# Divisions, readings and stores as operations of their own, and a new order for all operations, in an attention-and-FFN kernel

## The chip, the cores and the metric

The kernel runs on one core of a Trainium2 chip. The metric is the device time of one execution in microseconds (us), lower is better; of several runs the median is given. One core has a matrix engine (TensorE, PE in the profile, with its weight loads shown apart as PEld), three engines that work element by element (VectorE = DVE, ScalarE = ACT, GpSimd = POOL), and a sync engine (SP) that here only issues DMA transfers. Each engine executes its own instructions in program order. An instruction that needs a result of another engine waits on a semaphore, and everything behind it on its engine waits with it.

## The reference, cut to what matters

```python
# q, k, v: (8 batches, 8 heads, 576 positions, 64)
def phi(x, c, s):                          # c, s = cos, sin of pi/2 * position / 576
    r = np.maximum(x, 0.0)
    return np.concatenate([r * c, r * s], axis=-1)
q_p = phi(q, cos_w, sin_w)                 # 128 features
k_p = phi(k, cos_w, sin_w)
kv = np.einsum('bhsf,bhsd->bhfd', k_p, v)
z = np.sum(k_p, axis=2)
num = np.einsum('bhsf,bhfd->bhsd', q_p, kv)
den = np.einsum('bhsf,bhf->bhs', q_p, z)[..., None] + 1e-06
x = (num / den).transpose(0, 2, 1, 3).reshape(4608, 512)
h = x @ w_in                               # 512 -> 2048
out = np.maximum(0.01 * h, h) @ w_out      # 2048 -> 512
```

It is a linear attention (cosFormer), whose output is divided by a row sum, followed by a two-layer network with a leaky ReLU.

## The kernel before, in words

The 4608 tokens are worked in nine groups of 512: group g = 0 to 7 is the first 512 positions of batch g, group 8 gathers the 64 tail positions of all eight batches. A group goes through the same stages.

- *Attention.* q and k go through phi on DVE, ACT or POOL (`q_prep`, `k_cos`, `k_sin`; `q`, `k` in the first two groups). PE sums k_pᵀ[v|1] over positions (`kv_sum`; `kv` in the first groups). q_p is transposed, by PE or by a DMA (`q_transpose_dma`), and PE multiplies it with kv (`num(g,j)`, four blocks j of 128 tokens; `nh(b,jp,hg)` in the first two groups, half-blocks over token pair jp and head half hg). The product holds the numerator and, in one column per head, the denominator.
- *Division* (lines 571 to 576). Three DVE instructions: denominator plus 1e-6 (`den`), its reciprocal (`rden`), and numerator times reciprocal into the tile `xs`. They follow one another in one function `divide`, which `num` calls itself and `dh` calls for the half-blocks.
- *Transpose of x.* `xs` becomes `xT`, through PE in the first three groups (`xh`, `x_transpose`), through a DMA on SP's queue from group 3 on (`x_transpose_dma`, line 524).
- *FFN1.* Plain matmuls for groups 0 to 2 (`h`, `M`; line 634). From group 3 on a scheme with seven products in place of eight: `P(g,u,n)` is product n of column part u (line 787), `e(g,u,x)` are the steps that read the products and apply the leaky ReLU, `x_sum(g,i)` the sums of quarters of x that it needs (tiles X1, X2, X4, X1b).
- *FFN2.* Plain for group 0 (`f2(tt,lo,hi)`, line 661: token block tt, rows lo to hi of the 16 parts of the hidden width). From group 1 on seven products again: `F(g,i)` is half i of the seven products' halves, four matmuls of 128x256 each (line 904). `g_sum` are the sums of quarters of the hidden layer. When a product's last half is done, the same call reads it (lines 687, 923, 932: into t1, t2, t3 inside `ext`, or into the output tile `osb`) and issues the store of the finished quarter (`store_quarter`, line 963 and 968; for group 8's last quarters `store_tail`, line 954). Quarters have the product numbers 2, 4, 3 and 5.

PSUM (the matmul accumulators) is given out from four small pools; `osb` has four buffers. Loads are issued on SP's queue, as are the DMA transposes and the stores; half of group 8's stores go through ACT's queue.

What sets the order is one long text, `PROGRAM`: a list of some thousand operations with the engine letter of each (D, A, P). The kernel is built by calling the operations in that order, so each engine's instructions stand in the order of the text, and a semaphore joins what depends on one another across engines. `idle(n)` puts in n matmuls on a blank tile. w_in and w_out are loaded in parts and cast to 16 bits by `w1(i,c,n,engine)` and `w2(i,engine)`; `w2` part i covers hidden parts 4i to 4i+3. `load(...)` in the text is a transfer on SP's queue.

Of the kernel before, what the change touches and what calls it, by code (L numbers as in the profile page):

```python
# [9 lines left out]
dt = mybir.dt  # L10
# [3 lines left out]
P = 128  # L14
J = 4
# [10 lines left out]
q(0,0,0,4,D) q(0,1,0,4,D) q(0,2,0,4,D) q(0,3,0,4,A) q(0,0,4,8,D) q(0,1,4,8,D) q(0,2,4,8,P) q(0,3,4,8,A)  # L26
k(0,0,1,c,D) k(0,0,1,s,D) k(0,1,2,c,D) k(0,1,2,s,D) qT(0,0,A,h) idle(1,o) qT(0,1,A,h) idle(1,o) v(0,0,1,A)
v(0,1,2,A) qT(0,2,A,n) idle(1,o) qT(0,3,D,h) idle(6,o) kvps(0,h) kv(0,0,2) kvo(0,0,2,A) k(0,2,4,c,P,[0.1])
k(0,2,4,c,A,[1.9]) k(0,2,3,s,D) k(0,3,4,s,D) nh(0,0,0,h) dh(0,0,0) nh(0,1,0,n) dh(0,1,0) v(0,2,3,P) v(0,3,4,P)
idle(6,o) xh(0,0,0,o) xho(0,0,A,0,1) kvps(0,h) kv(0,2,4) kvo(0,2,4,A) w1(0,0,1,P) w1(0,1,1,P) w1(0,2,2,P)  # L30
w1(1,0,2,P) w1(1,2,2,P) w1(2,0,2,P) w1(2,2,2,P) w1(3,0,2,P) w1(3,2,2,P) xh(0,1,0) xho(0,0,A,1,2) nhps(0,0,1,h)
h(0,[0.1],[0],h,0,2) nh(0,0,1,-) dh(0,0,1) h(0,[0.1],[1],-,0,2) h(0,[0.1],[0.1],-,2,4) nh(0,1,1,n) dh(0,1,1)
xh(0,0,1,o) xho(0,1,A,0,1) h(0,[2.3],[0.1],h,0,2) h(0,[2.3],[0.1],-,2,4) xh(0,1,1) xho(0,1,A,1,2)
h(0,[0.1.2.3],[2.3],-,0,2) h(0,[0.1.2.3],[2.3],-,2,4) load(w2,0) load(w2,1) load(q,1) load(w2,2) load(k,1,0,2)
load(w2,3,0,2) load(v,1,0,2) load(w2,3,2,4) load(k,1,2,4) load(v,1,2,4) load(q,2) load(k,2) load(v,2)
h(0,[4.5],[0.1],n) h(0,[6.7],[0.1],h) h(0,[4.5.6.7],[2.3]) h(0,[8.9],[0.1.2.3],h) h(0,[10.11],[0.1.2.3],h)
w2(0,D) h(0,[12.13],[0.1.2.3],h) w2(1,D) h(0,[14.15],[0.1.2.3],h) q(1,0,0,8,D) q(1,1,0,8,D) q(1,2,0,8,D)
q(1,3,0,8,D) w2(2,D,0,2) w2(2,D,2,4) k(1,0,1,c,D) k(1,0,1,s,D) k(1,1,2,c,D) k(1,1,2,s,D) w2(3,D,0,2)
v(1,0,1,D) w2(3,D,2,4) f2(0,0,4) f2(1,0,4) f2(2,0,4) f2(3,0,4) f2(0,4,8) f2(1,4,8) qT(1,0,A,h) f2(2,4,8)
qT(1,1,A,h) f2(3,4,8) qT(1,2,A,h) f2(0,8,12) qT(1,3,A,h) f2(1,8,12) f2(2,8,12) v(1,1,2,A) kvps(1,h) kv(1,0,2)  # L40
f2(3,8,12) kvo(1,0,2,A) k(1,2,3,s,D) k(1,3,4,s,D) k(1,2,4,c,A,[0.7]) k(1,2,4,c,D,[7.9]) f2(2,12,14)
nh(1,0,0,h) dh(1,0,0) nh(1,1,0,h) dh(1,1,0) f2(2,14,16) v(1,2,3,P) v(1,3,4,A) f2(3,12,16) f2o(2,A) f2o(3,A)
kvps(1,h) kv(1,2,4) kvo(1,2,4,A) f2(1,14,15) xh(1,0,0,h) xh(1,1,0) f2(0,12,16) xho(1,0,D) f2o(0,A) nh(1,0,1,h)
f2(1,12,14) f2(1,15,16) f2o(1,A) dh(1,0,1) nh(1,1,1,n) dh(1,1,1) h(1,[0.1],[0.1],h) xh(1,0,1,o) xho(1,1,A,0,1)
h(1,[2.3],[0.1],h) xh(1,1,1) xho(1,1,A,1,2) h(1,[4.5],[0.1],n) h(1,[0.1.2.3.4.5],[2.3]) weight_sum(1)
v_pairs(2,2,4,D) v_pairs(2,0,2,D) q_prep(2,0,0,8,D) q_prep(2,1,0,8,D) load(q,3) M(1,6) M(1,7) M(1,8) M(1,9)
M(1,10) M(1,11) M(1,12) weight_sum(3) load(k,3) load(v,3,0,2) q_prep(2,2,0,8,D) q_prep(2,3,0,8,P)
g_sum(1,1,0,4) M(1,13) q_transpose_dma(2,0) g_sum(1,1,4,6) weight_sum(2) M(1,14) k_sin(2,6,A) g_sum(1,3,0,6)
weight_sum(4) k_sin(2,7,D) k_cos(2,4,D) k_sin(2,2,D) k_sin(2,0,D) k_sin(2,3,D) M(1,15) F(1,0) k_cos(2,3,P)
# [12 lines left out]
q_prep(4,3,0,8,A) g_sum(2,1,4,6) M(2,12) q_transpose_dma(4,0) q_transpose_dma(4,1) M(2,13) g_sum(2,3,0,6)
# [97 lines left out]
def kernel(  # L160
# [1064 lines left out]
```

## Time and profile before

| what | value |
|---|---|
| time, median of 3 runs | 272.31 us (272.24 to 273.06) |
| span of the profiled execution | 270.2 us |
| between span and median | 2.1 us |
| PE busy | 262.9 us, 97% |
| DVE busy | 206.9 us, 77% |
| ACT busy | 178.8 us, 66% |
| POOL busy | 129.0 us, 48% |
| DMA | 57.07 MB, mean 211 GB/s |

The profile shows one execution. The span runs from its first to its last recorded work; the profiled execution's own time is given only by that span, so the runs' median is set beside it. A row of the trace gives start, length, engine, source line, operation, the tile written and the tiles read (their numbers left out), the shapes, and in square brackets how long the engine had been idle and who ended the idle time. Adjacent like instructions are merged into one row with a count (x4). PEclk, the granted clock of TensorE, was 1.00 in every stretch that is shown. PE's matmuls are pipelined, so the length of a matmul's row is longer than the step from one to the next.

### The profile page before, as it was taken

Reading aid. Unit: us, or ns where it says so; the run is one execution under the profiler, and the core shown is the slowest. Engines: PE = TensorE matmul, PEld = TensorE weight load, DVE = VectorE, ACT = ScalarE, POOL = GpSimd, SP = SyncE. Lnnn points to the kernel's source line nnn. Section 1 sums busy time; section 2 is a strip of 40 time slices with the busy share of each in tenths; the row PEclk is TensorE's granted clock in tenths of the full one; section 3 lists DMA queues with packets and bytes.
Section 4 is the critical chain, followed back from the end, with each engine's and each line's share of the span. In section 5 each row is a group of like instructions: output and inputs, shape, how many; then the busy total and the mean of one; then the engine's idle time right before and its main releaser. Section 6 shows DMA issues by size and latency. Waiting matters only on the chain.

```text
span 270.2 us, 7060 instructions
## 1 busy us (share of the span) xinstructions
PE 262.9 (97%) x2877; PEld 218.2 (81%) x2877; DVE 206.9 (77%) x419; ACT 178.8 (66%) x312; POOL 129.0 (48%) x103
## 2 busy tenths in 40 slices
PE   7899999999999999999999999999999999999993
PEld 2585455557975599999999999999999899999983
DVE  4950597689967997997988789897789867757852
ACT  7857448478967877998688776776834564565500
POOL 2476000995879276979992869734130004000000
PEclk9999999999999999999999999999999999999999
DMA  6999999999999999789979993893565052111214
GB/s 225 370 395 411 383 398 371 375 298 257 304 201 302 213 216 379 244 127 292 241 150 203 256 359 101 145 219 67 126 150 119 2 116 81 39 41 39 80 39 118
DMA packets 75040, 57.07 MB, mean 211 GB/s; under 512 B 47232, under 2 KB 63616, under 8 KB 74624
## 3 DMA queue, kind: packets, MB, share of 16 engines
q1 hardware_dynamic: 74400, 56.11, 75.5%
q10 hardware_dynamic: 608, 0.52, 0.6%
q8 instruction: 22, 0.36, 0.6%
q14 instruction: 10, 0.08, 0.1%
HBM read 36.70 MB, written 9.44 MB: 171 GB/s over the span
## 4 chain that ended last, share of the span: by engine, by line
PE 93%; DMA 3%; ACT 1%; DVE 1%; SPq 1%; issue 0%
PE ps L904 35%; PE ps_f L787 27%; PE ps_h L634 15%; PE ps_o L661 5%; PE ps_num L560 3%; PE ps_kv L473 3%; DMA vst<-in_v_dram 3%; PE ps_f L904 1%; PE ps_xT L1077 1%; PE ps_kv L1004 1%; PE ps_numh L1055 1%; PE ps_qt L546 1%; PE ps_idle L338 0%; ACT vm L404 0%; SPq L260 0%; ACT qpT L404 0%
## 5 line engine op out<-in xcount | busy, mean ns | idle before, releaser
L904 PEld LDWEIGHTS <-g 128*128 128x128 f16 x640 | 61.8, 98 | 6.8
L904 PE MATMUL ps<-w,g 128*128 128x256 f16 x496 | 65.1, 273 | 0.0
L814 ACT ACTIVATE g<-ps_f 128x512 f16<-128x512 f32 x72 | 42.0, 598 | 19.1 <-PE ps_f L787 9.8
L634 PE MATMUL ps_h<-xT,w 128*128 128x512 f16 (+1 forms) x208 | 43.6, 363 | 0.0
L787 PEld LDWEIGHTS <-w 128*128 128x128 f16 x384 | 41.6, 114 | 0.7
L787 PE MATMUL ps_f<-xT,w 128*128 128x256 f16 x288 | 42.1, 273 | 0.0
L634 PEld LDWEIGHTS <-w 128*128 128x128 f16 x208 | 22.7, 114 | 16.2
L645 ACT ACTIVATE g<-ps_h 128x1024 f16<-128x1024 f32 x24 | 24.2, 1025 | 12.7 <-PE ps_h L634 12.7
L904 PE MATMUL ps<-T,ext 128*128 128x256 f16 x240 | 32.2, 273 | 0.0
L398 POOL TENSOR_SCALAR kp<-kst,cos_t 128x256 f16<-128x256 f32 (+1 forms) x21 | 29.9, 1430 | 4.7 <-DMA kst<-in_k_dram 4.7
L787 PEld LDWEIGHTS <-wext 128*128 128x128 f16 x288 | 31.3, 114 | 0.5
L904 PEld LDWEIGHTS <-ext 128*128 128x128 f16 x256 | 24.9, 98 | 2.5
L398 POOL TENSOR_SCALAR qp<-qst,cos_t 128x512 f16<-128x512 f32 (+1 forms) x10 | 19.5, 1951 | 10.0 <-DMA qst<-in_q_dram 5.3
L787 PE MATMUL ps_f<-X,wext 128*128 128x256 f16 x144 | 21.5, 273 | 0.0
L687 DVE TENSOR_TENSOR osb<-ps,ext 128x512 f32<-128x512 f32 x23 | 15.8, 688 | 6.5 <-PE ps L904 6.2
L687 DVE TENSOR_TENSOR ps_f<-ps_f,u 128x512 f32<-128x512 f32 x24 | 16.6, 693 | 5.0 <-PE ps_f L787 3.2
L576 DVE TENSOR_TENSOR xs<-ps_num,rden 128x512 f16<-128x512 f32 x28 | 19.4, 691 | 1.0
L398 POOL TENSOR_SCALAR kp<-kst,sin_t 128x256 f16<-128x256 f32 x15 | 18.6, 1247 | 2.3 <-PE ps_kv L473 2.3
L814 ACT ACTIVATE g<-y 128x512 f16<-128x512 f32 x24 | 15.2, 632 | 6.8 <-DVE y L687 6.7
L398 POOL TENSOR_SCALAR qp<-qst,sin_t 128x512 f16<-128x512 f32 (+1 forms) x10 | 19.1, 1912 | 0.0
L687 DVE TENSOR_TENSOR y<-ps_f,s 128x512 f32<-128x512 f32 x24 | 16.4, 684 | 1.4 <-PE ps_f L787 1.3
L687 DVE TENSOR_TENSOR ext<-g 128x512 f16<-128x512 f16 (+1 forms) x24 | 13.8, 576 | 3.8 <-ACT g L645 2.1
(122 smaller groups left out, 457.0 us busy)
## 6 DMA issues: line engine op xcount, KB each, us to landing
out_dram<-osb SPq DMA_DIRECT2D x32, 256.0 KB, 2.7
qst<-in_q_dram SPq DMA_DIRECT2D x7, 1024.0 KB, 11.7
kst<-in_k_dram SPq DMA_DIRECT2D x5, 1152.0 KB, 8.5
vst<-in_v_dram SPq DMA_DIRECT2D x5, 1152.0 KB, 8.4
w2st<-in_moe_w_out_dram SPq DMA_DIRECT2D x3, 1024.0 KB, 14.1
vst<-in_v_dram SPq DMA_DIRECT2D x4, 576.0 KB, 5.9
ext<-in_moe_w_in_dram SPq DMA_DIRECT2D x4, 512.0 KB, 10.7
kst<-in_k_dram SPq DMA_DIRECT2D x2, 576.0 KB, 6.5
```

The source lines that it names most:

```text
L398: eng.tensor_scalar(out=o, in0=i, scalar1=0.0, scalar2=col, op0=ALU.max, op1=ALU.mult)
L473: nc.tensor.matmul(ps[:, o, (c - lo) * NE : (c - lo + 1) * NE], lhsT=st["kp", b][sl, c, j, :], rhs=vm[sl, c, j, :], start=(j == 0), stop=( ...
L546: nc.tensor.transpose(ps[:, h, :], qp[:, h, :], ident)
L560: nc.tensor.matmul(ps[lo:hi, h // 4, (h % 4) * NE : (h % 4 + 1) * NE], lhsT=qpT[:, h, lo:hi], rhs=kv[b][:, h, :],)
L576: nc.vector.tensor_tensor(out=xs, in0=ps[:, :, 0 : 4 * NE].rearrange("p a (b e) -> p a b e", e=NE)[:, :, :, 0:D], in1=rden.rearrange("p (a ...
L634: nc.tensor.matmul(ps[:, m % 2, lo:hi], lhsT=w1[m // 4, c][0][:, w1[m // 4, c][1], m % 4 : 512 : 4], rhs=xT[:, lo // P : hi // P, c, :], s ...
L645: nc.scalar.activation(st["g", g][:, m - 1 : m + 1, :], ps, AF.Lrelu)
L661: nc.tensor.matmul(st["ps_o", g, tt], lhsT=st["g", g][:, m, tt * P : (tt + 1) * P], rhs=w2[:, m, :], start=(m == 0), stop=(m == NFT - 1),)
L687: eng.tensor_tensor(out=o, in0=a, in1=b, op=op)
L787: nc.tensor.matmul(ps[:, mi * HT : (mi + 1) * HT], lhsT=a[:, c, 2 * r0 + mi : 512 : 4], rhs=b[:, c], start=(n in (1, 5) and mi == 0 and c ...
L814: nc.scalar.activation(st["g", g][:, m : m + 2, r * HT : (r + 1) * HT], {"a": A, "c": y22, "e": E, "d": B_}[e].rearrange("p (m t) -> p m t ...
L904: nc.tensor.matmul(ps[:, tt], lhsT=a[:, i, tt * P : (tt + 1) * P], rhs=b[:, i], start=(first and i == 4 * halves[0]), stop=(i == NPR - 1 a ...
```

## The change

Three things become operations with places of their own in `PROGRAM`.

1. `divide` is split: `den`, `rec` and `mul` are three operations, each with its own place. `num` and `nh` only note where the product stands.
2. The reading of a finished FFN2 product is `R(g,n,engine)` and its store `S(g,n)` (for group 8's last quarters with the half tt as a third or fourth number). Before, both happened when the last half product had been issued.
3. The last sums of the hidden layer, which the code added by itself after the last FFN1 step of a group, are `g_sum` operations in the text.

All the text is written anew: order and engine letters. PE has the same 2877 matmuls, 29 idle fillers among them, and SP the same 110 transfers. POOL has 83 operations where it had 99, ACT 327 where it had 310, DVE 418 where it had 419. The first lines of the text and three others that later sections use:

```diff
-q(0,0,0,4,D) q(0,1,0,4,D) q(0,2,0,4,D) q(0,3,0,4,A) q(0,0,4,8,D) q(0,1,4,8,D) q(0,2,4,8,P) q(0,3,4,8,A)
+q(0,0,0,4,D) q(0,2,0,4,A) q(0,3,4,8,A) q(0,3,0,4,A) q(0,1,0,4,D) q(0,0,4,8,D) q(0,2,4,8,D) q(0,1,4,8,D) k(0,0,1,c,D)
...
-k(0,2,4,c,A,[1.9]) k(0,2,3,s,D) k(0,3,4,s,D) nh(0,0,0,h) dh(0,0,0) nh(0,1,0,n) dh(0,1,0) v(0,2,3,P) v(0,3,4,P)
+k(0,3,4,s,D) nh(0,1,0,n) nh(0,0,0,h) den(0,0,0) rec(0,0,0) mul(0,0,0) den(0,1,0) rec(0,1,0) kvps(1,h) nhps(0,0,1,h)
...
-w2(0,D) h(0,[12.13],[0.1.2.3],h) w2(1,D) h(0,[14.15],[0.1.2.3],h) q(1,0,0,8,D) q(1,1,0,8,D) q(1,2,0,8,D)
-v(1,0,1,D) w2(3,D,2,4) f2(0,0,4) f2(1,0,4) f2(2,0,4) f2(3,0,4) f2(0,4,8) f2(1,4,8) qT(1,0,A,h) f2(2,4,8)
+h(0,[8.9],[0.1.2.3],h) h(0,[12.13],[0.1.2.3],h) h(0,[14.15],[0.1.2.3],h) h(0,[10.11],[0.1.2.3],h) w2(1,D) w2(0,D)
+k(1,1,2,c,D) w2(3,D,0,2) f2(1,0,4) f2(2,0,4) f2(1,4,8) f2(0,0,4) f2(3,0,4) qT(1,0,A,h) f2(2,4,8) f2(3,4,8) qT(1,2,A,h)
...
-F(8,26) F(8,27)
+F(8,18) F(8,19) R(8,4,D) F(8,21) R(8,5,D,0) S(7,3) S(7,4) S(8,4) F(8,22) F(8,23) R(8,5,D,1) S(8,5,1) F(8,24) F(8,25)
+R(8,3,D,0) S(8,3,0) S(8,5,0) F(8,26) F(8,27) R(8,3,D,1) S(8,3,1)
```

The code:

```diff
-        divide(ps, st["xs", g][:, j].rearrange("p (a b) e -> p a b e", a=2))
-
-    def divide(ps, xs):
-        den = small.tile([P, H], dt.float32, name="den")
+        st["div", g, j] = ps, lambda: st["xs", g][:, j].rearrange("p (a b) e -> p a b e", a=2)
+
+    def den(*k):
+        ps, _ = st["div", *k]
+        st["den", *k] = d = small.tile([P, H], dt.float32, name="den")
         nc.vector.tensor_scalar_add(
-            den.rearrange("p (a b) -> p a b", a=2), ps[:, :, D : 4 * NE : NE], 1e-6
-        )
-        rden = small.tile([P, H], dt.float32, name="rden")
-        nc.vector.reciprocal(rden, den)
+            d.rearrange("p (a b) -> p a b", a=2), ps[:, :, D : 4 * NE : NE], 1e-6
+        )
+
+    def rec(*k):
+        st["rden", *k] = r = small.tile([P, H], dt.float32, name="rden")
+        nc.vector.reciprocal(r, st["den", *k])
+
+    def mul(*k):
+        ps, xs = st["div", *k]
...
         done.update(("f2", g, n, tt, half) for half in halves)
-        if apart and halves[-1] == 1:
+        st["psr", g, n] = ps
+        if apart:
+            st["psr", g, n, tt] = ps
+
+    def result(g, n, e, tt=None):
+
+        ps = st["psr", g, n]
+        lone, last = g == G7, g == NG - 1
+        eng = engines[e]
+        if tt is not None:
...
+            st["osb", g, n, tt] = osb = out_tile(g, HC)
+            tt_op(osb, st["psr", g, n, tt][:, tt], {5: t3, 3: t2}[n][:, part], ALU.add)
             return
...
+        if n == 1:
+            copy(eng, t1, flat)
+            return
+        if n in (6, 7):
+            tt_op({6: t2, 7: t3}[n], flat, t1, ALU.add)
+            return
+        st["osb", g, n] = osb = out_tile(g, 512)
+        if n == 2 and not lone:
+            copy(eng, osb, flat)
+        else:
             t = {2: t1, 5: t3, 4: t3 if lone or last else t1, 3: t2}[n]
-            result(g, n, lambda osb: tt_op(osb, flat, t, ALU.add))
+            tt_op(osb, flat, t, ALU.add)
+
+    def store(g, n, tt=None):
+        if tt is not None:
+            store_tail(2 * (n == 5) + tt, 1, st["osb", g, n, tt])
+            return
...
-            if u == 3 and e == "d":
-                for k in (1, 2):
-                    g_sum(g, k, 5, NPR, 2)
```

How the text moves instructions is seen on each engine. First, DVE in the opening, the first two divisions of group 0 (`ps_numh` is the product of numerator and denominator; 317 and 314 are the half-blocks that PE makes first, 331 and 323 those that it makes second). Before:

```order
L571 TENSOR_SCALAR den_326<-ps_numh_317 128x8
L575 RECIPROCAL rden_328<-den_326 128x8
L576 TENSOR_TENSOR xs_316<-ps_numh_317,rden_328 128x2x256
L571 TENSOR_SCALAR den_340<-ps_numh_331 128x8
L575 RECIPROCAL rden_342<-den_340 128x8
L576 TENSOR_TENSOR xs_316<-ps_numh_331,rden_342 128x2x256
```

Changed:

```order
L576 TENSOR_SCALAR den_332<-ps_numh_323 128x8
L582 RECIPROCAL rden_334<-den_332 128x8
L590 TENSOR_TENSOR xs_336<-ps_numh_323,rden_334 128x2x256
L576 TENSOR_SCALAR den_338<-ps_numh_314 128x8
L582 RECIPROCAL rden_340<-den_338 128x8
L590 TENSOR_TENSOR xs_336<-ps_numh_314,rden_340 128x2x256
```

DVE still divides half-block (0,0,0) first, but PE now makes it second.

Second, DVE in group 4: the division of the last of the four blocks, whose `mul` completes the tile that SP's transpose reads (`ps_f`, `y22`: steps of FFN1; `qp`: phi of q; `ext<-ps_7,ext`: the reading of a finished FFN2 product). Before:

```order
L687 TENSOR_TENSOR ps_f3_1610<-ps_f3_1610,u1_184 128x512
L687 TENSOR_TENSOR y22_186<-ps_f0_1607,s5_185 128x512
L571 TENSOR_SCALAR den_1951<-ps_num_1942 128x8
L575 RECIPROCAL rden_1953<-den_1951 128x8
L576 TENSOR_TENSOR xs_1819<-ps_num_1942,rden_1953 128x512
L398 TENSOR_SCALAR qp_1928<-qst_1639,cos_t_160 128x8x64
L398 TENSOR_SCALAR qp_1928<-qst_1639,sin_t_161 128x8x64
L687 TENSOR_TENSOR ext_96<-ps_7_1644,ext_96 128x512
```

Changed:

```order
L663 TENSOR_TENSOR ps_f3_1608<-ps_f3_1608,u1_184 128x512
L663 TENSOR_TENSOR y22_186<-ps_f0_1605,s5_185 128x512
L576 TENSOR_SCALAR den_1967<-ps_num_1945 128x8
L582 RECIPROCAL rden_1969<-den_1967 128x8
L663 TENSOR_TENSOR ext_96<-ps_7_1625,ext_96 128x512
L590 TENSOR_TENSOR xs_1837<-ps_num_1945,rden_1969 128x512
L663 TENSOR_TENSOR g_1385<-g_1385,ext_96 128x4x256
```

The reading of group 2's product 7 now stands between the reciprocal and the multiplication. A little later DVE has a sum that POOL had before: X1 of group 4, which waits for that transpose; behind it stand a sum of the hidden layer and the last reading of group 2. Changed:

```order
L663 TENSOR_TENSOR osb_2053<-ps_7_1625,ext_96 128x512
L663 TENSOR_TENSOR X1_180<-xT_2021 128x512
L663 TENSOR_TENSOR ext_96<-g_1600 128x2x256
L663 TENSOR_TENSOR osb_2074<-ps_7_1887,ext_96 128x512
L663 TENSOR_TENSOR ext_96<-g_1600 128x1024
L663 TENSOR_TENSOR X2_181<-xT_2021,X1_180 128x512
```

Third, SP's last stores (`osb` tiles; 64x2x256 and 64x256 are group 8's, 128x2x256 those of a group before). ACT's queue ends with the same order of group 8's halves. Before:

```order
L963 DMA out_0_dram<-osb_4142 128x2x256
L968 DMA out_0_dram<-osb_4203 64x2x256
L968 DMA out_0_dram<-osb_4242 64x2x256
L954 DMA out_0_dram<-osb_4254 64x256
L954 DMA out_0_dram<-osb_4266 64x256
L954 DMA out_0_dram<-osb_4278 64x256
L954 DMA out_0_dram<-osb_4290 64x256
```

Changed:

```order
L946 DMA out_0_dram<-osb_4213 64x2x256
L941 DMA out_0_dram<-osb_4179 128x2x256
L941 DMA out_0_dram<-osb_4123 128x2x256
L946 DMA out_0_dram<-osb_4244 64x2x256
L932 DMA out_0_dram<-osb_4264 64x256
L932 DMA out_0_dram<-osb_4276 64x256
L932 DMA out_0_dram<-osb_4250 64x256
L932 DMA out_0_dram<-osb_4290 64x256
```

The first half of quarter 5 (4254 before, 4250 now) has moved from the first of the four small stores to the third, and two stores of group 7 now stand among group 8's.

More of the change, by code (lines that the diff above doesn't have):

```diff
@@ L1168 @@
         "kvo": lambda b, lo, hi, e: kv_out(b, lo, hi, engines[e]),
-        "num": num_c,
         "nhps": num_ps,
         "nh": num_h,
-        "dh": div_h,
+        "den": den,
+        "rec": rec,
+        "mul": mul,
         "xh": xT_h,
```

327 lines of the change are left out of this document (132 added, 195 removed).

## The prediction

> **What bounds the kernel now.** I read the page's busy times, then the chain of work that ended last, then the busy times in three stretches (columns: stretch in us, its length, busy time of each engine and its instructions, granted TensorE clock, DMA share), then what TensorE waited for (total us, times, longest).
>
> ```profile
> PE 262.9 (97%) x2877; PEld 218.2 (81%) x2877; DVE 206.9 (77%) x419; ACT 178.8 (66%) x312; POOL 129.0 (48%) x103
> ...
> PE 93%; DMA 3%; ACT 1%; DVE 1%; SPq 1%; issue 0%
> ...
> 0.00:20.00 20.00, 16.88 (x210) 11.23 (x211) 12.51 (x35) 14.37 (x28) 9.83 (x21) 1.00 0.92 329
> 20.00:262.00 242.00, 242.00 (x2634) 203.64 (x2633) 192.02 (x379) 164.44 (x284) 119.15 (x83) 1.00 0.77 205
> 262.00:270.30 8.30, 4.02 (x37) 3.36 (x35) 2.39 (x5) 0.00 (x0) 0.00 (x0) 1.00 0.37 101
> ...
> PE ps_idle L338 <- DVE blank L333: 1.2, 1, 1.2
> PE ps_qt L546 <- DVE qp L398: 1.1, 1, 1.1
> PE ps_numh L1055 <- ACT kv L404: 0.5, 1, 0.5
> PE ps_xT L1077 <- DVE xs L576: 0.2, 1, 0.2
> PE ps_qt L546 <- POOL qp L398: 0.2, 1, 0.2
> ```
>
> From 20 to 262 us PE is busy 242.00 of 242 us at clock 1.00. Its five waits (1.2+1.1+0.5+0.2+0.2 = 3.2 us) all belong to operations of the opening. The changed kernel has the same 2877 matmuls, 29 of them idle fillers as before. So the middle can only stay or get longer: whatever was gained on DVE, ACT or POOL there ends in front of a PE that was never waiting. A gain has two places, the 3.2 us of the opening and what follows the last matmul.
>
> The opening hangs on a transfer. The chain begins with v landing; the rows behind it (start us, length, engine, line, operation, in square brackets the idle time before and who ended it) lead to the first division and from it back to PE.
>
> ```profile
> 2.33 7.40 DMA vst<-in_v_dram
> ...
> 9.76 1.25 ACT L404 CAST vm<-vst 128x576 f16<-128x576 f32 x2 [0.33 <-DMA vst<-in_v_dram]
> 12.25 0.67 PE L1055 MATMUL ps_numh<-kv,qpT 128*128 128x66 f16 x16 [0.47 <-ACT kv L404]
> 12.90 0.15 DVE L571 TENSOR_SCALAR den<-ps_numh 128x8 f32<-128x8 f32 x1
> 13.09 0.20 DVE L575 RECIPROCAL rden<-den 128x8 f32<-128x8 f32 x1
> 13.33 0.69 DVE L576 TENSOR_TENSOR xs<-ps_numh,rden 128x512 f16<-128x512 f32 x1
> 14.07 0.40 PE L1077 MATMUL ps_xT<-ident,xs 128*128 128x128 f16 x4
> ```
>
> The end: the last reading of a product on DVE, the two queues' final stores (64x256 each; the four of a queue merge into one row, its last issue has a row of its own), and the median time from an issue to its landing.
>
> ```profile
> 266.06 0.42 DVE L687 TENSOR_TENSOR osb<-ps_f,ext 128x256 f32<-128x256 f32 x1 [0.45 <-PE ps_f L904]
> ...
> 263.98 3.06 ACTq L954 DMA_DIRECT2D out_dram<-osb  x4
> ...
> 266.51 0.47 SPq L954 DMA_DIRECT2D out_dram<-osb  x1
> 266.52 0.52 ACTq L954 DMA_DIRECT2D out_dram<-osb  x1
> ...
> out_dram<-osb ACTq DMA_DIRECT2D x4, 64.0 KB, 2.2
> ```
>
> The last product is read by 266.48, the last store issued at 266.51; 266.52 + 2.2 = 268.7, and the rest to the span's 270.2 is the program's close. Either queue's last issue sets the end, since nothing stands behind it. The median of the runs shown is 272.31, so 2.1 us lie around the span of 270.2; I make the sum on the span and carry those 2.1 over.
>
> **The change part by part.** *Splitting the division.* No instruction is added: den, rec and mul stay one short and one 128x512 DVE operation each, with 0.15, 0.20 and 0.69 us above. Putting other work between them delays mul by that work. It is hidden wherever the next reader of xs, a transpose by DMA that is itself early, has slack; I cost it at nothing except in the opening and at group 4 below; where the cover is gone, a read of 0.69 put between costs its 0.69. A gain is excluded where PE waits nowhere.
>
> *Opening.* PE now makes the second numerator half-block (0,1,0) before (0,0,0), but DVE still divides (0,0,0) first. The 16 matmuls at 12.25 take 0.67 us and end at 12.92, so den starts at about 12.95 where it started at 12.90: +0.05, carried by mul, transpose and copies to the first FFN matmul. One q quarter goes from POOL to ACT (two activations more ahead of the v casts at 9.76, where ACT had 0.33 us idle) and DVE's half-blocks are reordered; ACT stays just ahead of v, so nothing is gained or lost there. Ends: 0 and +0.3 (ACT late for v). I take +0.05, nearest to the row.
>
> *w2.* The load and the cast of w_out's part 1 now come before part 0, but the first FFN2 products still read part 0. Columns as above; the last row is a piece of the chain.
>
> ```profile
> 27.01 1.23 DVE L406 CAST w<-w2st 128x2048 f16<-128x2048 f32 x1 [8.77 <-DMA w2st<-in_moe_w_out_dram]
> 29.66 1.23 DVE L406 CAST w<-w2st 128x2048 f16<-128x2048 f32 x1 [1.43 <-DMA w2st<-in_moe_w_out_dram]
> ...
> 30.86 5.18 PE ps_o L661 x24
> ```
>
> Before, PE at 30.86 needed the first cast (over at 28.24). Now it needs the second: 29.66 + 1.23 = 30.89, plus a handover. The only price is 30.89 against PE's arrival at 30.7 to 30.9: bounds 0 and +0.25, I take +0.15. A loss in the landing of the second transfer would go through whole.
>
> *Readings and stores apart.* A finished product's read is now an operation of its own and can stand later. What that may cost is a product whose accumulator is still unread when its next user comes. In group 3 half product F(3,24) stands eight matmuls behind the last one of the product that R(3,5,D) reads.
>
> ```profile
> 220.00:230.00 10.00, 10.00 (x94) 9.46 (x92) 7.63 (x14) 4.50 (x10) 3.60 (x3) 1.00 0.38 96
> ...
> L814 ACT ACTIVATE g<-ps_f 128x512 f16<-128x512 f32 x72 | 42.0, 598 | 19.1 <-PE ps_f L787 9.8
> L687 DVE TENSOR_TENSOR osb<-ps,ext 128x512 f32<-128x512 f32 x23 | 15.8, 688 | 6.5 <-PE ps L904 6.2
> ```
>
> A matmul takes 10.00/94 = 0.106 us, eight 0.85. The DVE read takes 0.688, an ACT read 0.598. With two handovers (PE to reader, reader to PE; in the opening's rows mul ends at 14.02 and PE starts at 14.07, so 0.05 or somewhat more each) the DVE read needs 0.80 to 0.90 and the ACT read 0.70 to 0.80: the first may stall PE by up to 0.1, the second just fits. One such DVE place: +0.1 (0 to 0.2). The same eight-matmul distance over an ACT read occurs at about 20 places instead of about 8; 12 more at 0 to 0.02 each: +0.1 (0 to 0.3).
>
> *Engines.* POOL gives up 16 operations, ACT gains 17, DVE loses one. Summed, 0.6 us per ACT operation is 10 us more on an engine that was busy 178.8 of 270. No engine becomes the bound by that; what matters is order.
>
> *The transpose of group 4.* Its four blocks are divided, then SP issues the transposing DMA.
>
> ```profile
> 114.50 0.69 DVE L576 TENSOR_TENSOR xs<-ps_num,rden 128x512 f16<-128x512 f32 x1
> 115.25 1.77 SPq L524 DMA_TRANSPOSE xT<-xs  x1
> 121.27 1.16 POOL L687 TENSOR_TENSOR X<-xT 128x512 f16<-128x512 f16 x1 [1.97 <-DMA xT<-xs]
> 122.15 0.60 PE L787 MATMUL ps_f<-xT,w 128*128 128x256 f16 x4
> ```
>
> Issued at 115.25, landed by 121.2, first read by PE at 122.15: about 0.9 us to spare. Now the reading R(2,7,D), 0.69, stands between rec and mul of the last block, and block and PE order shift, so the issue comes near 116.5 (115.25 + 0.69 + some 0.6 of order); landing near 122.4 at worst and 120.8 at the 4.3 us that such transposes take in the median, against a first reader that I place near 122.6, and against the sum X1, which now runs on DVE instead of POOL and is read four matmuls later. Ends 0 and +0.8. I take 0: at the median latency there is over a microsecond. This is the place with least cover, and what is behind it on DVE are group 3's sums and group 2's last reading.
>
> ```profile
> xT<-xs SPq DMA_TRANSPOSE x6, 4.3
> ```
>
> *Tail.* On both queues the first half store of quarter 3 is now followed by the first half store of quarter 5, which was ready long before, and only then by the last. On SP and ACT alike one issue more stands between the last two products. An issue takes 0.47 on SP and 0.52 on ACT; the half store ahead is ready 0.87 us (266.06 − 265.19) before the last one, so two issues of 0.5 or more end at or after it. SP then issues its last near 266.7, ACT near 266.8, where both had 266.5.
>
> ```profile
> 265.19 0.42 DVE L687 TENSOR_TENSOR osb<-ps_f,ext 128x256 f32<-128x256 f32 x1 [0.45 <-PE ps_f L904]
> ```
>
> From 265.19 + 0.42 = 265.61 the two issues end at 265.61 + 2 x 0.52 = 266.65, plus gaps. I take +0.3 (bounds 0 and +0.55, one whole issue). On DVE and PE the tail's last product comes no sooner.
>
> **The sum:** 0.05 + 0.15 + 0.1 + 0.1 + 0.3 = +0.7 us on the span: 270.2 + 0.7 = 270.9, and with 2.1 around it 273.0. That is 0.26% above 272.31, while about 0.3% (0.8 us, so 271.5 to 273.1) is what a measurement of this kernel can tell from no change. All lower ends together give 0, all upper ends 0.3 + 0.25 + 0.2 + 0.3 + 0.55 = +1.6 and with the transpose +2.4. They will not all go one way: I take the middle half of the first span, +0.4 to +1.2, as the sum's own range, 272.7 to 273.5.
>
> **The rivals.** *A stalled queue (slower).* One late transfer holds an engine that has other work behind the wait. The place is group 4: if X1 waits on DVE for a transpose that lands over 1.2 us later than I reckon, PE's second product of the group waits for it, and DVE's sums behind it come late too. For: 4.3 is a median, and the row above shows 6.0 us for this very transfer. Against: at those 6.0 it lands at 122.5 and still just fits. Similar places are ACT waiting for q or k of batch 7. From the point where the landing passes about 122.5 it costs PE one for one: 1 to 2 us at one place, twice that at two, so 273.5 to 276, middle 274.3.
>
> *The shared port (slower).* At the same place DVE works beside POOL.
>
> ```profile
> 115.03 1.99 POOL L398 TENSOR_SCALAR qp<-qst,sin_t 128x512 f16<-128x512 f32 x1
> 115.11 0.89 DVE L398 TENSOR_SCALAR qp<-qst,cos_t 128x512 f16<-128x512 f32 x1
> 115.91 0.47 DVE L398 TENSOR_SCALAR qp<-qst,sin_t 128x512 f16<-128x512 f32 x1
> ```
>
> Beside the same POOL operation one DVE operation takes 0.89 and the next 0.47: at most 0.42 us of hindrance, and only now and then. If X1, on DVE in the changed kernel while POOL prepares q, were held for a whole POOL operation of 1.99 us, it would pass the reader's 122.6 by about 1.7 us: 272.3 + 0.7 + 1.7 = 274.7. The row speaks against this. The Trainium skill, "SBUF — State Buffer", section "Who interferes with whom", says that VectorE and GpSimd share a pair of ports under an exclusive lock, so that a two-input DVE operation and a GpSimd operation that reads SBUF block one another for the whole instruction. By that rule the place would cost those 1.7 us; the trace does not agree here, since 0.89 ends long before the POOL operation's 117.02.
>
> *Hidden anyway (no change).* PE reaches FFN2 late enough, the queues take the extra store in their gaps, the reads fit: only +0.05 to +0.1, 272.4. For: each of the terms is smaller than half a microsecond and has a lower end of nothing.
>
> *Faster.* The opening's q reorder lets PE's first transposes and with them the whole chain start up to 1.1 us sooner, the wait of ps_qt. Against: the division hangs on v's landing at 9.73 and not on q. Even 1.1 us is told from no change only if the losses above stay hidden too: 272.3 − 1.1 + 0.1 = 271.3.
>
> **How the numbers follow.** The sum holds in 0.58 of cases; as it lies at the edge, 0.36 fall inside 0.3% and 0.22 above it. Stalled queue 0.24, port 0.04, hidden 0.08, faster 0.06. So faster 0.06, same 0.36 + 0.08 = 0.44, slower 0.22 + 0.24 + 0.04 = 0.50. I predict the sum, 273.0. The range for 8 in 10 goes from 272.2 (leaving out the faster case and a little of the hidden one) to 275.0 (leaving out the third of the stalls that cost two places).
>
> **What the profile after would show.** Right: PE busy all through 20 to 260 us but for tenths; a row of ps_o waiting for DVE's w near 30.9 with at most 0.25; den of the first division some 0.05 later; the last stores issued 0.2 to 0.5 after the last reading ends, on both queues; xT of group 4 issued about 116.5. Wrong: a row of PE waiting for X, xT, ext or a DMA with a microsecond or more (stalled queue); X1 with 2 us on DVE (port); last issue within 0.1 of the reading (hidden); the first division before 12.5 (faster).

## The result and the profile after

| | before | changed |
|---|---|---|
| median | 272.42 us (272.11 to 273.06, 7 runs) | 274.2 us (273.1 to 275.4, 7 runs) |
| ratio | 1 | 1.0064 (95% interval 1.0044 to 1.0084) |
| span of the profiled execution | 270.2 us | 272.6 us |

The change makes the kernel slower by 0.64%, 1.8 us, where 273.0 (+0.26%) was forecast. The time lies inside the forecast range of 272.2 to 275.0, but above the sum's own range of 272.7 to 273.5: of the cases it is the rival "a stalled queue". In every run for which both are given, time less span is about 1.8 us (1.74 to 1.86) and not the 2.1 of the prediction. The profiled execution of the kernel before (span 270.2) was thus one of about 272.0, faster than its median, and the two profiled executions lie 2.4 us apart where the medians lie 1.8 apart. The shares below are read from the profiles.

The same views as before, of the changed kernel: first the page's busy times,

```profile
PE 264.1 (97%) x2877; PEld 218.0 (80%) x2877; DVE 201.3 (74%) x418; ACT 184.7 (68%) x329; POOL 109.2 (40%) x87
```

then the chain of work by engine,

```profile
PE 78%; DMA 15%; ACT 3%; SPq 2%; DVE 1%; issue 0%; POOL 0%; ACTq 0%
```

then the three stretches,

```profile
0.00:20.00 20.00, 16.82 (x207) 10.97 (x208) 12.43 (x35) 15.08 (x30) 6.99 (x19) 1.00 0.92 328
20.00:262.00 242.00, 240.90 (x2616) 201.58 (x2615) 184.62 (x376) 169.08 (x298) 102.26 (x69) 1.00 0.73 202
262.00:273.00 11.00, 6.38 (x59) 5.46 (x56) 4.21 (x7) 0.58 (x1) 0.00 (x0) 0.89 0.52 143
```

and what PE waited for (five of eight rows, those that the kernel before did not have).

```profile
PE ps_f L763 <- DVE y L663: 0.4, 1, 0.4
PE ps_kv L982 <- DVE kp L1063: 0.4, 1, 0.4
PE ps_kv L482 <- POOL vm L415: 0.3, 1, 0.3
PE ps_num L566 <- DMA qpT<-qp: 0.3, 1, 0.3
PE ps_kv L982 <- POOL vm L415: 0.2, 1, 0.2
```

(The clock of 0.89 belongs to the time after PE's end at 268.38; up to 270 us it is 1.00.) In the middle PE is no longer busy 242.00 of 242 us but 240.90, and the transfers' share of the chain has risen from 3% to 15%. The waits are new ones, each in front of data that a transfer brings, some of them through an engine in between. The matmuls' overlap hides part of a wait in these rows, and the wait for DVE's kp (0.4) lies in front of the first kv matmul. The true gap is how much longer the step from one matmul's start to the next is than usual; measured so from that matmul on, there are five that the kernel before does not have, of 0.38, 0.26, 0.49, 0.43 and 0.59 us, 2.15 us together. From the first kv matmul to the end of the last matmul the changed kernel takes 257.42 us (10.96 to 268.38), the kernel before 254.99 (11.03 to 266.02): 2.43 more.

*Gap 1, the opening.* POOL casts a part of w1 between the two halves of v, and that part has not landed. Rows of POOL, then of PE:

```profile
12.62 0.85 POOL L415 CAST vm<-vst 128x576 f16<-128x576 f32 x1 [0.60 <-DMA vst<-in_v_dram]
13.78 0.61 POOL L415 CAST w<-w1st 128x512 f16<-128x512 f32 x1 [0.32 <-DMA w1st<-in_moe_w_in_dram]
14.34 0.67 POOL L415 CAST vm<-vst 128x576 f16<-128x576 f32 x1
...
15.06 0.46 PE L982 MATMUL ps_kv<-vm,kp 64*128 64x66 f16 x18 [0.21 <-POOL vm L415]
```

v's last half, landed long before, is ready at 15.01 where the kernel before had it at 14.12.

*Gap 2, w2,* as forecast: the second cast is over at 31.27, and the first ps_o product starts at 31.32.

```profile
30.04 1.23 DVE L415 CAST w<-w2st 128x2048 f16<-128x2048 f32 x1 [1.33 <-DMA w2st<-in_moe_w_out_dram]
31.32 1.02 PE L637 MATMUL ps_o<-w,g 128*128 128x512 f16 x4
```

*Gaps 3 and 4, batch 3.* In the kernel before the load of q (1 MB, for batch 4) left at 64.92:

```profile
64.92 0.75 SPq L260 DMA_DIRECT2D qst<-in_q_dram  x1
```

Here it left at 68.18, directly ahead of the second half of v(3), and 4 us ahead of the transpose of q(3,0). SP's queue in order, then the readers:

```profile
68.18 0.79 SPq L269 DMA_DIRECT2D qst<-in_q_dram  x1
69.01 1.26 SPq L283 DMA_DIRECT2D vst<-in_v_dram  x1
72.42 5.29 SPq L519 DMA_TRANSPOSE qpT<-qp  x1
...
77.92 1.14 POOL L415 CAST vm<-vst 128x1152 f16<-128x1152 f32 x1 [3.13 <-DMA vst<-in_v_dram]
79.11 0.75 PE L482 MATMUL ps_kv<-vm,kp 64*128 64x66 f16 x36 [0.32 <-POOL vm L415]
81.11 0.43 PE L566 MATMUL ps_num<-kv,qpT 128*128 128x66 f16 x8 [0.26 <-DMA qpT<-qp]
```

v(3) takes 8.9 us from issue to landing (5.9 before) and the transpose 8.64 (7.12 before).

*Gap 5, batch 6.* k of batch 6 is issued at 126.07 and lands at 133.3. In the kernel before it was issued at 123.10:

```profile
123.10 0.43 SPq L274 DMA_DIRECT2D kst<-in_k_dram  x1
```

In the changed kernel ACT waits for it with a step of FFN1's reading behind that wait; DVE's y needs that step, and PE's next product needs y.

```profile
126.07 0.93 SPq L283 DMA_DIRECT2D kst<-in_k_dram  x1
133.37 0.51 ACT L405 ACTIVATE kp<-kst,cos_t 128x256 f16<-128x256 f32 x1 [0.82 <-DMA kst<-in_k_dram]
133.78 0.61 ACT L790 ACTIVATE g<-y 128x512 f16<-128x512 f32 x1
134.43 0.69 DVE L663 TENSOR_TENSOR y<-ps_f,s 128x512 f32<-128x512 f32 x1 [0.70 <-ACT g L790]
135.17 0.60 PE L763 MATMUL ps_f<-X,w 128*128 128x256 f16 x4 [0.43 <-DVE y L663]
```

Three engines stand in a row behind one transfer that PE itself doesn't need for a long time.

### The profile page after: what moved, and what is told of

Same layout as the page of the kernel before. It is cut to its first block, busy times and chain, and to the rows that moved or that the text cites. A ratio compares the mean times of both kernels' runs of the same rounds, so it can differ in the third digit from the quotient of the medians.

```text
span 272.6 us, 7039 instructions
## 1 busy us (share of the span) xinstructions
PE 264.1 (97%) x2877; PEld 218.0 (80%) x2877; DVE 201.3 (74%) x418; ACT 184.7 (68%) x329; POOL 109.2 (40%) x87
## 4 chain that ended last, share of the span: by engine, by line
PE 78%; DMA 15%; ACT 3%; SPq 2%; DVE 1%; issue 0%; POOL 0%; ACTq 0%
PE ps L877 30%; PE ps_f L763 25%; PE ps_h L613 10%; PE ps_o L637 5%; DMA w2st<-in_moe_w_out_dram 5%; DMA w1st<-in_moe_w_in_dram 4%; DMA qpT<-qp 3%; DMA kst<-in_k_dram 3%; PE ps_num L566 2%; PE ps_kv L482 1%; ACT qp L405 1%; PE ps_f L877 1%; ACT kp L405 1%; SPq L283 1%; PE ps_qt L555 1%; PE ps_kv L982 0%
## 5 line engine op out<-in xcount | busy, mean ns | idle before, releaser
L877 PE MATMUL ps<-T,ext 128*128 128x256 f16 x240 | 33.7, 273 | 0.0
L407 POOL TENSOR_SCALAR qp<-qst,cos_t 128x512 f16<-128x512 f32 x8 | 17.2, 2156 | 16.0 <-DMA qst<-in_q_dram 7.1
L407 POOL TENSOR_SCALAR kp<-kst,cos_t 128x256 f16<-128x256 f32 (+1 forms) x12 | 17.7, 1482 | 9.4 <-DMA kst<-in_k_dram 9.4
L407 POOL TENSOR_SCALAR kp<-kst,sin_t 128x256 f16<-128x256 f32 x15 | 19.4, 1296 | 3.5 <-PE ps_f L763 3.5
L877 PE MATMUL ps<-ext,g 128*128 128x256 f16 x128 | 17.3, 273 | 0.0
L413 ACT COPY ps_f<-ps_f 128x512 f32<-128x512 f32 x22 | 12.6, 574 | 6.5 <-PE ps_f L763 4.7
L413 ACT COPY u<-ps_f 128x512 f32<-128x512 f32 x15 | 8.8, 589 | 10.7 <-PE ps_f L763 10.6
```

The costliest lines, as they stand in the source:

```text
L407: eng.tensor_scalar(out=o, in0=i, scalar1=0.0, scalar2=col, op0=ALU.max, op1=ALU.mult)
L413: nc.scalar.copy(o, i)
L877: nc.tensor.matmul(ps[:, tt], lhsT=a[:, i, tt * P : (tt + 1) * P], rhs=b[:, i], start=(first and i == 4 * halves[0]), stop=(i == NPR - 1 a ...
```

## The experiments

The theory was that these five places make up the loss (theory 1), the rivals that the split itself costs time everywhere (theory 2) or that the tail's stores do (theory 3). One run of these kernels differs from another by half a microsecond and more, so each experiment is read in the profile as well, by its gaps and by the stretch from the first kv matmul to the end of the last matmul (254.99 before, 257.42 changed). The ratio in parentheses is taken over all runs of a kernel against the kernel before, with its 95% interval, and is not quite the ratio of the medians. The gaps that an edit does not touch vary from execution to execution as well, so a stretch's change is not the edited gaps alone.

### Opening put back

```diff
-v(0,2,3,P) w1(0,0,1,P) v(0,3,4,P)
+v(0,2,3,P) v(0,3,4,P) w1(0,0,1,P)
...
-load(w2,1) load(w2,0)
+load(w2,0) load(w2,1)
...
-w2(1,D) w2(0,D)
+w2(0,D) w2(1,D)
```

> The changed kernel with two places of the opening put back: the cast w1(0,0,1) behind the two v casts on POOL, and w2 part 0 loaded and cast before part 1. Theory 1 (time is lost where one engine stands in front of a transfer and others wait behind it, and in each of five places of the profile by the PE gap seen there): the gap of 0.38 us in the second kv sum near 14.7 us and the gap of 0.26 us before the first ps_o product go away, and the span falls by 0.3 to 0.6 us against the changed kernel's 274.2, to 273.6 to 273.9. Theory 2 (the split itself, more separate instructions and semaphores everywhere): nothing moves, 274.2. Theory 3 (the reordered stores of the tail): nothing moves, 274.2.

274.24 us (ratio to the kernel before 1.0071, 1.0046 to 1.0097): no gain in time. In its profile gaps 1 and 2 are gone, but PE, now earlier, waits for v(3) all the longer; the kv sum's second half starts at 79.20, the changed kernel's at 79.11. What PE waited for:

```profile
PE ps_kv L482 <- POOL vm L415: 1.0, 1, 1.0
```

The gap there grew from 0.49 to 1.19 us. The opening's 0.64 were given back there, at a transfer of the middle (gap 5 is 0.17 in this execution, and the stretch 257.12): the expected 273.6 to 273.9 missed this, since it took the gaps as independent.

### The load of q(4) behind the transpose

```diff
-rec(2,0) mul(2,0) load(q,4) k_sin(3,1,A)
+rec(2,0) mul(2,0) k_sin(3,1,A)
...
-mul(2,2) q_transpose_dma(3,0)
+mul(2,2) q_transpose_dma(3,0) load(q,4)
```

> The changed kernel with the load of q for batch 4 issued behind the transpose of q(3,0) instead of before the second half of v(3): it no longer has 1 MB ahead of those two transfers. Theory 1: v(3) lands before its cast is due and the transpose lands about 3 us sooner, so the gaps of 0.49 us (kv sum of batch 3, near 78.6) and 0.43 us (num(3,0), near 80.5) both go; 273.2 to 273.5 against 274.2, unless q(4) itself now comes late to ACT. If the gaps come from the order of operations and not from the bytes ahead, they stay. Theories 2 and 3: 274.2.

273.57 us (1.0052, 1.0034 to 1.0071). Gaps 3 and 4 are gone and POOL no longer waits for v(3); the stretch falls by 1.3 to 256.15. The two gaps are 0.92 of that; gap 1 is absent too in this execution, in which the first kv matmul started 0.42 us later (11.38).

```profile
68.46 0.78 SPq L283 DMA_DIRECT2D vst<-in_v_dram  x1
...
75.04 1.19 POOL L415 CAST vm<-vst 128x1152 f16<-128x1152 f32 x1
```

### What held SP: q_prep(2,2)

Why had the load left 3.3 us late? In SP's queue it stands behind the transpose of q(2,1), which needs `q_prep(2,2)`. The change gave that to ACT, which does it between two readings of FFN1's products and ends at 63.60 where DVE had ended at 59.22; the transpose left at 63.67 and 60.41. The last rows of it, in the changed kernel and in the kernel before:

```profile
62.89 0.71 ACT L405 ACTIVATE qp<-qst,sin_t 128x512 f16<-128x512 f32 x1
```

```profile
58.74 0.48 DVE L398 TENSOR_SCALAR qp<-qst,sin_t 128x512 f16<-128x512 f32 x1
```

Two kernels change one letter, one in the changed kernel, one in the kernel before:

```diff
-q_prep(2,2,0,8,A)
+q_prep(2,2,0,8,D)
```

> The changed kernel with one letter changed back: q_prep(2,2) on DVE instead of ACT. Theory 1: SP's transpose of q(2,1) and with it the load of q(4) leave up to 3 us sooner, the gaps at kv(3) (0.49) and num(3,0) (0.43) go, as they did when the load was moved behind; from the first kv matmul to the last 256.3 to 256.7 where the changed kernel has 257.4; 273.1 to 273.5. If another wait holds SP there, the gaps stay and the time is 274.2.

273.97 us (1.0059, 1.0036 to 1.0081, 4 runs), higher than expected. The load leaves at 65.73, both gaps are gone, and the stretch is 256.24.

```diff
-q_prep(2,2,0,8,D)
+q_prep(2,2,0,8,A)
```

> The kernel before with one letter changed: q_prep(2,2) on ACT instead of DVE, as in the changed kernel. Theory 1 (it is ACT's later place that holds SP's queue at the transpose of q(2,1), so that the load of q(4) comes 3 us later and lies ahead of v(3) and the transpose of q(3,0)): SP's transpose leaves near 63.6 instead of 60.4, v(3) and the transpose land 1 to 2 us later, and PE gets a gap of 0.3 to 1 us at kv(3) or num(3,0); from the first kv matmul to the last matmul 255.3 to 256.0 where the kernel before has 255.0; time 272.4 to 273.1. If it is the load's place in the text and not the queue's hold, nothing moves: 272.1.

272.65 us against 272.38 (1.001, 0.9995 to 1.0025). In time that is no difference that the runs can tell. SP's load leaves at 67.44 and the gap comes up in the kernel before, 0.89 us at kv(3); num(3,0) has none. The stretch is 256.56, longer by 1.57 and more than expected: 0.35 of it is a wait for a sum of x near 98 us.

```profile
67.44 0.78 SPq L251 DMA_DIRECT2D qst<-in_q_dram  x1
...
78.00 1.14 POOL L397 CAST vm<-vst 128x1152 f16<-128x1152 f32 x1 [1.34 <-DMA vst<-in_v_dram]
79.19 0.75 PE L464 MATMUL ps_kv<-vm,kp 64*128 64x66 f16 x36 [0.72 <-POOL vm L397]
```

One letter, on an engine that is not the bound, sets when a load behind a transpose in SP's queue starts. Five kernels show it for the gap at kv(3): it is there where q_prep(2,2) is on ACT and the load of q(4) also stands ahead of v(3) (the changed kernel and this one). It is not there with q_prep(2,2) on DVE (the kernel before, and the changed kernel with the letter put back), though the load stands ahead of v(3), nor with the load moved behind.

### k(6): the wait moved, or the transfer

```diff
-k_cos(6,2,A) e(4,0,c) k_cos(6,3,A)
+e(4,0,c)
...
-k_cos(6,5,D) e(4,1,y) rec(5,0) mul(5,0) e(4,1,e)
+e(4,1,y) rec(5,0) mul(5,0) e(4,1,e) k_cos(6,2,A) k_cos(6,3,A) k_cos(6,5,D)
```

> The changed kernel with three operations that read k of batch 6 (two on ACT, one on DVE) moved behind the last reading steps of the column part in work there, so that ACT doesn't wait for that transfer with e-steps behind it. Theory 1: the 0.59 us gap near 134.5 (PE waits for DVE's y, which waits for ACT's g, which stands behind the wait for k) goes; 273.5 to 273.8 against 274.2. If the gap only moves, to kv(6) or to num(6,0), the time stays. Theories 2 and 3: 274.2.

```diff
-q_transpose_dma(5,1) load(k,6)
+load(k,6) q_transpose_dma(5,1)
```

> The changed kernel with the load of k(6) issued before the transpose of q(5,1) on SP instead of behind it, and ACT's order left as it is. Theory 1 (ACT waits for this transfer with the reading steps behind it): issued 2 us sooner, k(6) lands about 2 us sooner than the 133.3 of the changed kernel and the gap of 0.59 us near 134.5 goes without any move on ACT or DVE; 273.6 to 274.0. If the gap came from ACT's order alone (too many operations ahead of the step that y waits for), it stays: 274.2.

In both profiles the gap near 134.5 is gone; with the sooner load POOL uses k(6) from 131.72 on. The stretches are 257.00 and 256.61, 0.4 and 0.8 less than 257.42; in the second 0.38 of that is gap 1, absent there because the first kv matmul started 0.40 us later (11.36). The times are 274.58 (1.0092, 1.006 to 1.0123) and 274.18 (1.0077, 1.0049 to 1.0105), no better than the changed kernel's 274.2. So the mechanism is shown and a gain in time by this repair alone is not. Both times lie above what was expected; the runs of these two reach up to 276.45, and what they wait for in those runs no profile shows.

### All repairs, and the tail

> The changed kernel with the edits of the three kernels beside it together. Theory 1: the five gaps are 0.38 + 0.26 + 0.49 + 0.43 + 0.59 = 2.15 us in the profile, and without them the time is the kernel before's, 272.0 to 272.7. Theory 2: 273.5 or more, since the split is still there. Theory 3: what remains over the kernel before is the tail's 0.3 to 0.5: 272.6 to 273.0.

273.27 us (1.0035, 1.0006 to 1.0065), slowest run 275.31. The time lies in none of the three expected ranges. In the profile none of the five gaps is left; the stretch is 255.43. In the opening of this execution v and k landed 1.3 us later than in the kernel before's. The first piece of its chain, and PE's longest wait:

```profile
2.33 8.74 DMA vst<-in_v_dram
```

```profile
PE ps_kv L982 <- DVE kp L1063: 1.9, 1, 1.9
```

Besides, the tail's store was put back:

```diff
-S(8,3,0) S(8,5,0) F(8,26)
+S(8,3,0) F(8,26)
...
-F(8,21) R(8,5,D,0) S(7,3) S(7,4) S(8,4) F(8,22)
+F(8,21) R(8,5,D,0) S(7,3) S(7,4) S(8,4) S(8,5,0) F(8,22)
```

> The three repairs of the changed kernel together, and besides the first half store of quarter 5 issued as soon as it is read, as in the kernel before. Theory 1 with a tail that costs nothing: last stores issued within 0.1 us of the last reading instead of 0.4 (SP) and 0.7 (ACT) behind it, yet from the last matmul's end to the end of the span 4.2 us as in all kernels so far, and 272.0 to 272.8 in time. Theory 3 (tail as predicted): that stretch becomes 3.8 to 3.9 us, 0.3 to 0.4 less than with the changed tail.

272.08 us (271.76 to 274.63, 12 runs) against 272.38: ratio 1.0004 (0.9985 to 1.0023). The loss is gone. PE in the middle:

```profile
20.00:262.00 242.00, 242.00 (x2632) 203.28 (x2630) 187.05 (x378) 169.73 (x299) 101.58 (x69) 1.00 0.73 202
```

The stretch is 255.28, and from PE's end to the end of the span it takes 3.81 us with this tail where the kernel with all other repairs takes 4.24. The step from 1.0035 to 1.0004 is larger than those 0.43 us (0.0016), and the two intervals overlap: what the tail is worth is read from the profiles, not from these times.

### The tail and the split alone

Written with the new operations in the old places, each engine's instructions are those of the kernel before, one for one. Only the quarter's store is moved:

```diff
-R(8,5,D,0) S(8,5,0) F(8,22)
+R(8,5,D,0) F(8,22)
...
-R(8,3,D,0) S(8,3,0) F(8,26)
+R(8,3,D,0) S(8,3,0) S(8,5,0) F(8,26)
```

> The order and engines of the kernel before, written with the new separate operations, and one thing moved: the first half store of quarter 5 stands behind the first half store of quarter 3, as in the changed kernel. If the split itself costs time (theory 2), it is slower than before by 1 us or more. If the moved store costs the 0.4 us that the repaired kernels showed between their two tails (4.24 and 3.81 us from PE's end to the span's end), that stretch becomes 4.6 where the kernel before has 4.2, and the time 272.7 to 272.9. If the kernel before already pays for issuing its two last stores at one moment (it has 4.2 and not 3.8 with them 0.03 us behind the reading), the stretch stays at 4.2 and the time at the kernel before's 272.1 to 272.5.

272.76 us against 272.45 (1.0005, 0.9988 to 1.0022). Theory 2, by which it would have cost 1 us or more, is out. The stores, SP and ACT, and the last reading, which ends at 266.69:

```profile
264.97 2.66 SPq L931 DMA_DIRECT2D out_dram<-osb  x4
264.98 2.95 ACTq L931 DMA_DIRECT2D out_dram<-osb  x4
266.27 0.42 DVE L662 TENSOR_TENSOR osb<-ps_f,ext 128x256 f32<-128x256 f32 x1 [0.45 <-PE ps_f L876]
```

The last issues end at 267.63 and 267.93, 0.9 and 1.2 us behind the reading (0.5 and 0.6 in the kernel before), and from PE's end to the span's end it takes 4.73 us where the kernel before has 4.21. The landings in the traces split that stretch in two. From PE's end to the landing of the last store it takes 2.70 to 2.74 us in all six kernels with the old place of the store, the kernel before among them, and 3.14 to 3.17 in all eight with the moved one, the changed kernel among them. So the moved store costs 0.43 us in either text. From the last landing to the span's end it takes 1.07 to 1.14 us in ten kernels, but 1.49 to 1.58 in the other four: the kernel before, this one and the two with w2 alone and with fewer fillers. These four have a pause of 0.36 to 0.39 us among the first six instructions with which SP closes; in the others no pause there is over 0.06. The changed kernel lacks the pause (1.08 against 1.49), and that hid the store between the two profiles: 4.21 and 4.24 from PE's end to the span's end. Where the pause comes from is open.

### w2 alone, and two tries at the opening

```diff
-load(w2,0) load(w2,1)
+load(w2,1) load(w2,0)
...
-w2(0,D)
+w2(1,D)
...
-w2(1,D)
+w2(0,D)
```

> The kernel before with the load and the cast of w2 part 1 ahead of part 0, and the products in their old order. Theory 1 and the prediction's own term: PE waits 0.15 to 0.3 us before its first ps_o product near 30.9; 272.2 to 272.5 against 272.1, below what the time alone can tell, so the gap in the profile decides.

272.55 us against 272.38 (1.0003, 0.9991 to 1.0016). PE waits for DVE's w as expected, but in this execution for longer:

```profile
PE ps_o L652 <- DVE w L397: 0.8, 1, 0.8
```

The gap was 1.01 us here and 0.25 to 0.40 in five other kernels with the swap: its size follows the second transfer's landing in that execution.

Two kernels tried to win time, one on the repaired kernel with DVE's k operations in pair order, one on the kernel before with four fillers fewer.

```diff
-k(0,0,1,c,D) k(0,1,2,c,D) k(0,1,2,s,D) k(0,0,1,s,D)
+k(0,0,1,c,D) k(0,0,1,s,D) k(0,1,2,c,D) k(0,1,2,s,D)
```

> The repaired kernel with the old tail, and in the opening the four k operations on DVE ordered pair by pair (cos and sin of the first head pair, then of the second), so that PE can start on the first half of the first kv sum while DVE still works on the second. In its profile PE waited 0.7 us for DVE's kp there. Theory 1 (the opening's chain goes straight through to the end, since PE never waits later): the first kv sum ends 0.3 us sooner and so does everything: 271.7 to 271.9, 0.1 to 0.25% under the kernel before. If what follows waits for transfers instead (v's second half, w1, w2), the gain ends there: 272.1.

```diff
-idle(6,o) kvps(0,h) kv(0,0,2)
+idle(2,o) kvps(0,h) kv(0,0,2)
```

> The kernel before with two idle fillers instead of six in front of the first kv sum, four fewer matmuls in all: the first half of that sum no longer stands behind them. Theory 1: it starts 0.4 us sooner and ends 0.3 us sooner; 271.8 to 272.1 against 272.1 to 272.4, unless v's second half (landing near 12.7, cast until 14.1) then holds PE. If TensorE's granted clock falls for want of fillers, slower by 1 us or more and seen in the clock column.

273.1 us (1.0023, 1.0006 to 1.0039) and 272.37 (1.0012, 0.9992 to 1.0032): no gain; the first was expected at 271.7 to 271.9. The kv sum starts sooner (10.84 and 10.69 us, where the kernels they vary have 11.25 and 11.03), but its first half now waits for ACT's cast of v, which waits for v's landing, and its second for DVE's k. PE's wait for ACT's kv grew from 0.5 to 0.7 us, and the products behind it start 2.51 us after v's landing in both, where they had started after 2.57 and 2.52. The opening's chain is the transfer's, as the prediction read it. With four fillers fewer the granted clock stays at 1.00 up to 265 us. No kernel here is faster than the kernel before; the repaired one equals it.

## Why the prediction was right and wrong

**Right: the frame.** That the middle can only get longer held in all kernels: the best reached 242.00 of 242 again, and no stretch was shorter than the kernel before's 254.99. The range held the time because it took in the rival of a stalled queue; the sum did not get there: of the five gaps' 2.15 us it has only w2's 0.26. That stalls at other places than the one named added up to the rival's size is luck.

**Right: w2.** +0.15 (0 to 0.25) was put down, 0.26 measured, the mechanism as told; with the swap alone it was 1.01 in one execution, by a later landing, which the prediction allows for.

**Half right: the tail.** +0.3 (0 to 0.55) was put down for the extra issue; it costs 0.43 to the last landing. The step "the rest to the span's 270.2 is the program's close", taken as fixed, failed: the close behind the last landing is 1.49 us in the kernel before and 1.08 in the changed one, so between the two profiles the term vanished.

**Half right: the opening.** The swapped half-blocks cost about what was put down, 0.05: den starts 0.70 to 0.72 us behind the first numerator product in all profiles with the new order, 0.61 to 0.65 with the old. In the changed kernel's profile the first kv matmul came 0.07 sooner, so den stood at 12.88 and not at 12.95. The larger loss, gap 1, is missing from the prediction. It looked for "ACT late for v"; it was POOL, with a cast in front of v that waits for its own transfer. The trace of before shows that landing, at 13.43, behind v's at 12.74.

**Not told apart: the readings and the round trips.** At F(3,24) PE starts at 147.00 behind a reading that ends at 146.95; no gap above 0.06 us stands there. Of the 2.43 us in the stretch the five gaps leave 0.28, in which the two terms of 0.1 would have to lie. The kernel with the old order and the new operations took 0.24 more than the kernel before in its execution, so it may also be nothing.

**Wrong: the transfers.** The step that failed is that the sum has no term for a late transfer but w2's ("I take 0", for group 4): gaps 3 to 5 are 1.5 of the 2.15 us. The place named, the transpose of group 4, just fitted: issued at 117.88, not 116.5, and X1 on DVE began at 123.39 with PE's first reader at 123.74. The stalls were at three other places, of 0.43 to 0.59 us and none of the microsecond that was to be the sign; v(3) and the transpose of q(3,0) do not occur in the prediction. The rival had the mechanism and 273.5 to 276, but neither the place nor the size of one stall; "ACT waiting for q or k of batch 7" came near gap 5, which is k of batch 6. What was not worked out is how far one queue hands on a delay: an operation moved to a later engine, the transpose that waits for it, and all loads behind that in SP's queue.

**The port rival did not happen.** X1 ran beside a POOL operation that reads SBUF and was not held:

```profile
121.02 3.38 POOL L407 TENSOR_SCALAR kp<-kst,sin_t 128x256 f16<-128x256 f32 x3
123.39 0.61 DVE L663 TENSOR_TENSOR X<-xT 128x512 f16<-128x512 f16 x1
125.46 0.41 DVE L663 TENSOR_TENSOR X<-xT,X 128x512 f16<-128x512 f16 x1
```

By POOL's row its last operation runs until 124.40; X1 is over at 124.00, 0.2 us longer than its like at 125.46. The prediction's own row against the rival was no test of it, since it shows a DVE operation with one tensor input. The Trainium skill, "SBUF — State Buffer", section "Who interferes with whom", calls the ports that VectorE and GpSimd share an exclusive lock, and has a VectorE operation with two inputs in SBUF contend with a GpSimd operation that reads SBUF. For X1 the trace does not agree: it was slower, not blocked. But that depends on POOL's operation. In the 14 traces 483 sums of this shape on DVE (128x512, 16 bits, two inputs) ran with no POOL operation beside them, and none took over 0.43 us. 302 began inside a TENSOR_SCALAR of POOL: 58 took over 0.5 us, the longest 0.91. 24 began inside a TENSOR_TENSOR of POOL, and all 24 ended 0.28 to 0.29 us after it. One of these, in the kernel before:

```profile
96.10 1.27 POOL L687 TENSOR_TENSOR X<-xT,X1b 128x512 f16<-128x512 f16 x1 [6.81 <-DVE X1b L687]
96.40 1.26 DVE L687 TENSOR_TENSOR ext<-ext,g 128x512 f16<-128x512 f16 x1
```

For two such sums the traces do agree with a lock. So the rival has a case beside a sum on POOL, but at X1 POOL prepares k. POOL's rows are rough in their spans; that all 24 distances agree speaks for them here.

## What to carry to other kernels

In a kernel whose bound engine never waits in the middle, reorder with the transfers in mind: for each operation that changes engine, ask which transfer waits for it, and what stands behind that transfer in the same queue. An operation that waits for a transfer belongs behind what other engines need from its engine, not in front of it. Repairs of such stalls don't add up, since PE that comes sooner waits longer at the next late transfer (0.49 us became 1.19). None of the three alone was clear of the changed kernel's 1.0064 (1.0071, 1.0052 and 1.0092); all together gave 1.0035, and with the tail's 1.0004, no longer told from the kernel before.

## What the runs showed of the hardware

- The first kv matmul, which hangs on v's and k's landing, started between 10.69 and 12.40 us in the profiles of these kernels. One execution had v landed after 8.74 us where another took 7.40, with the same loads ahead: that alone is more than any one term of the sum.
- A transpose of q by DMA, issued 4.2 us behind a load of 1 MB, took 8.64 us from issue to landing; the 14 of that kernel took 4.2 to 9.0, with a median of 4.7.
- From the last store's landing to the end of the span it took 1.07 to 1.14 us in ten traces and 1.49 to 1.58 in four, with the same four last stores on each queue.
- A 128x512 sum of two 16-bit tensors on DVE took 0.41 us. Each of the 24 that began while POOL had such a sum ended 0.28 to 0.29 us after POOL's; beside POOL's TENSOR_SCALAR most kept their 0.41.
